# The first four heads of k through ScalarE's load queue as fp32, cast on VectorE

## The chip, the cores and the metric

The kernel runs on one core of a Trainium2 chip. The metric is the device time of one execution in microseconds (us). A profile of one execution gives, for every instruction, its engine, start and length; its span is some 1.8 us shorter than the time (572.4 us of span in a run of 574.16 us). Engines are named as in the profile: PE is TensorE's matmul side, PEld its weight load, DVE is VectorE, ACT is ScalarE, POOL is GpSimd, SP is SyncE. L147 is line 147 of the kernel.

## The reference, cut to what matters

Linformer attention over 8 batches of 8 heads (1024 tokens, head dimension 64, keys and values projected to 64 rows by E and F), then a SwiGLU feed-forward block over the 8192 resulting rows.

```python
k_proj = np.einsum('ks,bhsd->bhkd', E, k)
v_proj = np.einsum('ks,bhsd->bhkd', F, v)
scores = q @ k_proj.transpose(0, 1, 3, 2) / 8
attn = softmax(scores) @ v_proj
x = attn.transpose(0, 2, 1, 3).reshape(B * S, H * D)
out = (silu(x @ w_gate) * (x @ w_val)) @ w_out
```

## The kernel before

Everything arrives as fp32 and is computed in bf16. The loads on GpSimd's queue are cast in flight ("the casting queue" below); those on SyncE's and ScalarE's queues are not ("the hardware queues"). A load has landed when the last of its sixteen completions is there. After the first half batch of attention, PE runs the feed-forward part without a break and slips the other batches' attention in between. What matters here is the opening, before that stretch begins:

```python
load_k(0, 0, 4)                       # casting queue: heads 0 to 3 of k
for which, src in (("E", E), ("F", F)):
    nc.sync.dma_start(out=raw[:], in_=src)      # fp32, hardware queue of SyncE
...
load_k(0, 4, 8); load_q(0, 0, 2); load_v(0, (0, 4, 8)); load_w_gv(0, 1) ...   # casting queue
warm(8)                               # matmuls on zeros
turn(0)                               # transposes E on PE, ScalarE casts it to ET
turn(1)                               # transposes F on PE, VectorE casts it to FT
warm(7)
u_KV(0, "k", (0, 4), at="y")          # E times the first half of k
warm(2)
u_KT(0, at="v", prs=(0, 2))           # transposes the product
warm(2)
u_KV(0, "k", (4, 8), at="y")          # E times the second half of k
...                                   # transposes of q, scores, softmax on VectorE and GpSimd
u_KV(0, "v", (0, 4), at="y"); ... u_KV(0, "v", (4, 8), at="y")
...                                   # attention times v, then the first feed-forward matmuls
```

`warm(n)` issues n matmuls on zeros into a bank of PSUM (the memory that PE writes its results to) of the group "v". Its purpose is to keep TensorE's clock up while PE waits. PE executes all of this in program order.

The softmax here doesn't subtract the row's maximum and nothing guards it: scores larger than these inputs give would overflow.

Of the kernel before, what the change touches and what calls it, by code (L numbers as in the profile page):

```python
# [12 lines left out]
BF16 = mybir.dt.bfloat16  # L13
FP32 = mybir.dt.float32

B = 8
H = 8
S = 1024
D = 64
# [3 lines left out]
P = 128  # L23
NJ = S // P
# [10 lines left out]
def kernel(  # L35
# [19 lines left out]
    nc = tc.nc  # L55
# [4 lines left out]
    kv_pool = ctx.enter_context(tc.tile_pool(name="kv", bufs=2))  # L60
    q_pool = ctx.enter_context(tc.tile_pool(name="qbf", bufs=4))
    aw = ctx.enter_context(tc.tile_pool(name="aw", bufs=2))
# [20 lines left out]
    kb, vb, qb, xT, hT = {}, {}, {}, {}, {}  # L83

    def load_k(b, h0=0, h1=H):
        if h0 == 0:
            kb[b] = kv_pool.tile([P, H, NJ, D], BF16, name="kb", tag="kb")
        nc.gpsimd.dma_start(  # L88
            out=kb[b][:, h0:h1].rearrange("p h j d -> p h (j d)"),
            in_=k[b, h0:h1].rearrange("h (p j) d -> p h (j d)", j=NJ),  # L90
        )

    def load_v(b, heads=(0, H)):
        t = kv_pool.tile([P, H, NJ, D], BF16, name="vb", tag="vb")
        vb[b] = t
        for h0, h1 in zip(heads, heads[1:]):
            nc.gpsimd.dma_start(
                out=t[:, h0:h1].rearrange("p h j d -> p h (j d)"),
                in_=v[b, h0:h1].rearrange("h (p j) d -> p h (j d)", j=NJ),
            )  # L100
# [11 lines left out]
    def load_w_gv(c0, c1, which=(0, 1)):  # L112
        cs = slice(c0 * P, c1 * P)
        for wsrc, wdst in [((moe_w_gate, wg), (moe_w_val, wv))[i] for i in which]:
            nc.gpsimd.dma_start(
                out=wdst[:, :, cs],
                in_=wsrc[:, cs].rearrange("(t p) c -> p t c", p=P),
            )
# [11 lines left out]
    def bank(where, shape, dt, name):  # L130
        pool, tag = banks[where]
        return pool.tile(shape, dt, name=name, tag=tag)

    def copy(eng, out, in_):
        (nc.scalar.copy if eng is nc.scalar else eng.tensor_copy)(out=out, in_=in_)  # L135
# [51 lines left out]
    def u_T(b, u, at="a", eng=nc.scalar):  # L187
        ch, w = divmod(u, 4)
        g, i = divmod(w, 2)
        ps = bank(at, [P, 4, P], BF16, "qTp")  # L190
        src = qb[b, ch]
        for n in range(4):
            nc.tensor.transpose(  # L193
                out=ps[:, n, :],
                in_=src[:, 4 * g + n, 2 * i : 2 * i + 2, :].rearrange("p j d -> p (j d)"),
                identity=ident_bf[:],
            )
        t = aw.tile([P, 4, P], BF16, name="qT", tag="qT", bufs=4)
        copy(eng, t[:], ps[:])
        qT[b, u] = t  # L200
# [46 lines left out]
    def u_N(b, u):  # L247
        ch, w = divmod(u, 4)
        g, i = divmod(w, 2)
        if (b, ch) in BY_DMA:  # L250
            if (b, ch, "d") not in AA:
                AA[b, ch, "d"] = aw.tile([P, 4, H, KP], BF16, name="AAd", tag="AAd")
            a = AA[b, ch, "d"][:, 2 * i : 2 * i + 2, 4 * g : 4 * g + 4, :]
        else:
            a = AA[b, u] = aw.tile([P, 2, 4, KP], BF16, name="AA", tag="AA", bufs=4)
            a = a[:]
        eng = nc.vector if b == 0 and u in (2, 3) else nc.gpsimd
        eng.tensor_tensor(  # L258
            out=a.rearrange("p j h k -> p h j k"),
            in0=ee.pop((b, u))[:],  # L260
            in1=rr.pop((b, u))[:].unsqueeze(3).to_broadcast([P, 4, 2, KP]),
            op=ALU.mult,
        )
# [160 lines left out]
            fn(*a)  # L424

    with tc.manual_schedule():
        load_k(0, 0, 4)
        ef = []
        for which, src in (("E", E), ("F", F)):
            raw = const.tile([KP, S], FP32, name=f"{which}raw")  # L430
            nc.sync.dma_start(out=raw[:], in_=src)
            ef.append(raw)
        zeros = const.tile([P, CW], BF16, name="zeros")
        nc.vector.memset(zeros[:], 0.0)
        make_identity(nc, ident_fp[:])
        make_identity(nc, ident_bf[:])
        for i in range(2):
            nc.vector.memset(BD[i][:], 0.0)
            nc.vector.memset(BDV[i][:], 0.0)

        def turn(which):
            for half in range(2):
                ps = bank("v", [P, 4, KP], FP32, "efp")
                for i in range(4):
                    j = 4 * half + i
                    nc.tensor.transpose(
                        out=ps[:, i, :],
                        in_=ef[which][:, bass.ds(j, P, step=NJ)],
                        identity=ident_fp[:KP, :KP],
                    )  # L450
                js = slice(4 * half, 4 * half + 4)
                copy((nc.scalar, nc.vector)[which], (ET, FT)[which][:, js, :], ps[:])

        def warm(n):

            ps = bank("v", [P, CW], FP32, "warm")
            for _ in range(n):
                nc.tensor.matmul(
                    out=ps[:], lhsT=zeros[:, 0:P], rhs=zeros[:],
                    start=True, stop=True,  # L460
                )


        load_k(0, 4, 8)
        load_q(0, 0, 2)
        load_v(0, (0, 4, 8))
        load_w_gv(0, 1)
        load_w_gv(1, 2)
        load_w_gv(2, 4)
        warm(8)  # L470
        turn(0)
        turn(1)
        warm(7)
        u_KV(0, "k", (0, 4), at="y")
        warm(2)
        u_KT(0, at="v", prs=(0, 2))
        warm(2)
        u_KV(0, "k", (4, 8), at="y")
        warm(2)
        u_KT(0, at="v", prs=(2, 4))  # L480
        u_T(0, 0, "a", nc.scalar)
        u_T(0, 1, "a", nc.vector)
        u_T(0, 2, "a", nc.scalar)
        u_S(0, 0, "g")
        u_T(0, 3, "v", nc.vector)
        u_S(0, 2, "g")
        u_S(0, 1, "a")
        u_S(0, 3, "a")
        u_R(0, 0)
        u_N(0, 0)  # L490
        u_R(0, 2)
        u_N(0, 2)
        load_w_gv(4, 6, (0,))
        u_KV(0, "v", (0, 4), at="y")
        warm(1)
        u_A(0, 0, nc.scalar)
        u_R(0, 1)
        u_N(0, 1)
        u_R(0, 3)
        u_N(0, 3)  # L500
        u_A(0, 2, nc.scalar)
        u_KV(0, "v", (4, 8), at="y")
        load_w_gv(4, 6, (1,))
        load_q(0, 1)
        load_w_gv(6, 8)
        load_w_gv(8, 10)
        load_w_gv(10, 12)
        load_wo(0)
        load_wo(1)
        load_k(1)  # L510
        warm(1)
        u_PV2(0, 0, 0, 0, nc.scalar)
        u_PV2(0, 0, 1, 0, nc.vector)
        u_A(0, 1, nc.scalar)
        u_A(0, 3, nc.vector)
        f_mm(0, 0, 0, 0)
        f_mm(0, 0, 1, 0)
        u_PV2(0, 0, 0, 1, nc.scalar)
        u_PV2(0, 0, 1, 1, nc.vector)
        f_mm(0, 1, 0, 0)  # L520
        f_mm(0, 1, 1, 0)

        for i, u in enumerate(range(4, 8)):
            put(12 + i, u_T, 0, u)
            put(14 + i, u_S, 0, u)
            put(15 + i, u_R, 0, u)
            put(15 + i, u_N, 0, u)
            put(19 + i, u_A, 0, u, nc.scalar)
        put(21, u_PV, 0, 1, 0)
        put(22, u_PV, 0, 1, 1)  # L530
        put(23, u_PV, 0, 1, 2)
        put(23, u_PV, 0, 1, 3)
        put(20, load_q, 1, 0)
        put(20, load_v, 1)
        put(20, load_q, 1, 1)
        for b in range(1, B):
            place(b)
        for b in range(2, B):
            s0 = 48 * (b - 1) - (12 if b == 2 else 24)
            put(s0, load_k, b)  # L540
            put(s0 + 2, load_v, b)
            put(s0 + 4, load_q, b, 0)
            put(s0 + 6, load_q, b, 1)

        for s in slots:
            slots[s].sort(key=lambda x: x[0] not in (load_k, load_v, load_q))


        ypart = defaultdict(list)
        for c in range(B * CH - 1):  # L550
            for n in range(NFT):
                f = n if c else 4 + (2 * n + 1) // 3
                ypart[(c + 1) * NFT + f].append((c, n))

        for t in range(NIT):
            c, f = divmod(t, NFT)
            i = 1 if t < 2 else None
            f_g(c, f, i)
            run_slot(2 * t)
            f_v(c, f, i)  # L560
            for a in ypart.pop(t, ()):
                f_y(*a)
            run_slot(2 * t + 1)
        for n in range(9):
            f_y(B * CH - 1, n)
        f_y_last(B * CH - 1, 3)
        assert not slots and not ypart
# [29 lines left out]
```

## Time and profile before

| | before |
|---|---|
| time, median of the first 3 runs | 573.41 us |
| span of the profiled run | 572.4 us |
| PE busy | 98% |
| first k matmuls / second k matmuls start | 9.74 / 12.29 us |
| second half of v lands, its matmuls start | 20.01, 20.05 us |
| first feed-forward matmuls start | 22.57 us |

The lines behind these rows are in the prediction below. The first feed-forward matmuls (`gps<-xT,wg`) start at 22.57 us, and from there to the end of the span it is 572.4 - 22.57 = 549.8 us.

### The profile page before, as it was taken

What the parts mean: (1) busy time and instruction counts of PE and PEld (TensorE: products, weight loads), DVE (VectorE), ACT (ScalarE), POOL (GpSimd) and SP (SyncE); (2) the same over time, 40 slices, a digit from 0 to 9 for tenths busy, and PEclk for the clock granted to TensorE, in tenths of its full rate; (3) what the DMA queues carried; (4) which work ended last, traced back from release to release, by engine and by line L of the source; (5) the groups of instructions that cost most, each with busy time, mean ns of one, the idle gap of its engine ahead of it and who ended that gap; (6) DMA issues with size and microseconds to landing.
All of it is one profiled execution on the core that took longest, in us unless ns stands there. A gap on an engine that the chain in (4) does not pass through costs nothing.

```text
span 572.4 us, 7867 instructions
## 1 busy us (share of the span) xinstructions
PE 561.2 (98%) x2910; PEld 268.6 (47%) x2967; DVE 336.8 (59%) x580; ACT 237.0 (41%) x416; POOL 107.9 (19%) x121
## 2 busy tenths in 40 slices
PE   8899999999999999999999999999999999999997
PEld 4654544444444444444444444444444444444444
DVE  2787566666466744766556665567546674554550
ACT  1655444353425434444335434354342543443232
POOL 6734131234002400124001330023200220000000
PEclk9999999999999999999999999999999999999999
DMA  9999993539901698037951399204990124100012
GB/s 160 196 200 206 201 161 74 93 64 196 201 37 41 110 190 157 18 75 129 187 108 38 59 179 195 63 22 88 197 176 37 42 52 74 38 37 25 31 39 92
DMA packets 105927, 61.34 MB, mean 107 GB/s; under 512 B 58016, under 2 KB 97696, under 8 KB 105888
## 3 DMA queue, kind: packets, MB, share of 16 engines
q0 software_dynamic: 42288, 29.89, 36.1%
q1 hardware_dynamic: 63312, 30.68, 25.1%
q8 instruction: 23, 0.38, 0.3%
q10 hardware_dynamic: 288, 0.26, 0.1%
q14 instruction: 16, 0.13, 0.1%
HBM read 60.29 MB, written 16.78 MB: 135 GB/s over the span
## 4 chain that ended last, share of the span: by engine, by line
PE 94%; DMA 2%; POOL 1%; ACT 1%; issue 1%; DVE 0%; POOLq 0%
PE yps L360 29%; PE vps L322 29%; PE gps L322 29%; PE kvp L147 3%; PE sc L227 2%; DMA vb<-in_v_dram 2%; PE pv L285 2%; PE aTp L274 0%; ACT xT L135 0%; PE qTp L193 0%; POOL kb L88 0%; PE kTp L172 0%; POOL qb L107 0%; ACT th L334 0%; PE pv L300 0%
## 5 line engine op out<-in xcount | busy, mean ns | idle before, releaser
L341 DVE SCALAR_TENSOR_TENSOR s<-th,gps 128x512 f32<-128x512 f32 x192 | 130.5, 680 | 138.0 <-ACT th L334 137.8
L322 PE MATMUL gps<-xT,wg 128*128 128x512 bf16 (+1 forms) x755 | 195.7, 377 | 1.2
L322 PE MATMUL vps<-xT,wv 128*128 128x512 bf16 (+1 forms) x761 | 195.9, 377 | 0.8
L360 PE MATMUL yps<-wo,hT 128*128 128x512 bf16 (+2 forms) x761 | 191.5, 376 | 0.8
L334 ACT ACTIVATE th<-gps 128x512 f32<-128x512 f32 x192 | 114.6, 597 | 162.6 <-PE gps L322 155.1
L346 DVE TENSOR_TENSOR hT<-s,vps 128x512 bf16<-128x512 f32 x192 | 132.0, 688 | 22.1 <-PE vps L322 1.5
L360 PEld LDWEIGHTS <-hT 128*128 128x128 bf16 x780 | 76.2, 98 | 89.9
L258 POOL TENSOR_TENSOR AAd<-ee,rr 128x512 bf16<-128x512 f32 x52 | 54.1, 1040 | 319.5 <-issue 168.4
L322 PEld LDWEIGHTS <-wv 128*128 128x128 bf16 x776 | 73.9, 98 | 82.9 <-issue 3.3
L322 PEld LDWEIGHTS <-wg 128*128 128x128 bf16 x776 | 74.0, 98 | 81.3 <-issue 0.6
L370 ACT ACTIVATE ysb<-yps 128x512 f32<-128x512 f32 (+1 forms) x65 | 38.4, 590 | 78.1 <-PE yps L360 74.4
L135 ACT CAST xT<-pv 128x512 bf16<-128x512 f32 x62 | 36.1, 585 | 51.3 <-PE pv L285 50.3
L242 DVE TENSOR_REDUCE zz<-ee 128x8 f32<-128x512 f32 x64 | 43.5, 679 | 17.9 <-ACT ee L231 17.9
L231 ACT ACTIVATE ee<-sc 128x512 f32<-128x512 f32 x64 | 37.9, 595 | 17.4 <-PE sc L227 17.4
L285 PE MATMUL pv<-AT,BDV 128*128 128x512 bf16 x60 | 22.6, 379 | 0.1
L227 PEld LDWEIGHTS <-qTd 128*128 128x128 bf16 x208 | 16.0, 98 | 12.3
L227 PE MATMUL sc<-BD,qTd 128*128 128x128 bf16 x208 | 20.1, 219 | 0.1
L135 DVE CAST BDV<-kvp 64x256 bf16<-64x256 f32 x14 | 6.0, 426 | 22.1 <-ACT ks L157 19.1
L258 POOL TENSOR_TENSOR AA<-ee,rr 128x512 bf16<-128x512 f32 x10 | 10.3, 1038 | 35.2 <-DVE rr L244 33.6
L147 PE MATMUL kvp<-kb,ET 128*64 128x512 bf16 (+1 forms) x72 | 15.5, 357 | 1.3 <-DMA kb<-in_k_dram 1.3
L244 DVE RECIPROCAL rr<-zz 128x8 f32<-128x8 f32 x64 | 13.0, 203 | 6.2
L147 PE MATMUL kvp<-vb,FT 128*64 128x512 bf16 (+1 forms) x72 | 15.5, 358 | 1.0 <-DMA vb<-in_v_dram 1.0
(49 smaller groups left out, 144.8 us busy)
## 6 DMA issues: line engine op xcount, KB each, us to landing
out_dram<-ysb SPq DMA_DIRECT2D x63, 256.0 KB, 2.3
qb<-in_q_dram POOLq DMA_DIRECT2D x15, 512.0 KB, 16.6
kb<-in_k_dram POOLq DMA_DIRECT2D x7, 1024.0 KB, 11.6
vb<-in_v_dram POOLq DMA_DIRECT2D x7, 1024.0 KB, 14.2
wo<-in_moe_w_out_dram POOLq DMA_DIRECT2D x2, 768.0 KB, 14.8
wg<-in_moe_w_gate_dram POOLq DMA_DIRECT2D x5, 256.0 KB, 10.4
wv<-in_moe_w_val_dram POOLq DMA_DIRECT2D x5, 256.0 KB, 10.4
kb<-in_k_dram POOLq DMA_DIRECT2D x2, 512.0 KB, 8.7
```

What stands on the lines that cost most here:

```text
L135: (nc.scalar.copy if eng is nc.scalar else eng.tensor_copy)(out=out, in_=in_)
L147: nc.tensor.matmul(out=t[lo : lo + 64, h0:h1].rearrange("p h d -> p (h d)"), lhsT=w[:, j, :], rhs=src[b][:, h0:h1, j, :], start=(j == 0), ...
L227: nc.tensor.matmul(out=ps[:, n, :], lhsT=t[:, n, :], rhs=BD[b % 2][:, 4 * g + n, :], start=True, stop=True)
L231: nc.scalar.activation(out=e[:].rearrange("p h j k -> p (h j k)"), in_=ps[:].rearrange("p a k -> p (a k)"), func=AF.Exp, scale=scale,)
L242: nc.vector.reduce_sum(out=z[:], in_=e[:], axis=AX.X)
L258: eng.tensor_tensor(out=a.rearrange("p j h k -> p h j k"), in0=ee.pop((b, u))[:], in1=rr.pop((b, u))[:].unsqueeze(3).to_broadcast([P, 4, 2 ...
L322: nc.tensor.matmul(out=ps[:, ts], lhsT=(wg, wv)[w][:, kt, f * P : (f + 1) * P], rhs=x[:, kt, ts], start=(kt == 0), stop=(kt == NKT - 1),)
L334: nc.scalar.activation(out=th[:], in_=ps[:], func=AF.Tanh, scale=0.5)
L341: nc.vector.scalar_tensor_tensor(out=s1[:], in0=th[:], scalar=1.0, in1=g[:], op0=ALU.add, op1=ALU.mult)
L346: nc.vector.tensor_tensor(out=hT[c][:, f, :], in0=s1[:], in1=ps[:], op=ALU.mult)
L360: nc.tensor.matmul(out=yy[c][:, cs], lhsT=hT[c][:, f, i * P : (i + 1) * P], rhs=wo[:, f, cs], start=(f == 0), stop=(f == NFT - 1),)
L370: nc.scalar.activation(out=ysb[:, cs], in_=yy[c][:, cs], func=AF.Copy, scale=0.5)
```

## The change

The intent is to take one of the casting queue's chunks off that queue. Heads 0 to 3 of k are read raw, as two fp32 loads on ScalarE's queue, at the same moment as E and F on SyncE's. VectorE casts them. The casting queue starts with heads 4 to 7, so everything in it should come one chunk earlier. The waits of PE should shrink with that, so seven warming matmuls are taken out of them; three are put in further on.

```diff
-        load_k(0, 0, 4)
         ... (the tile kb[0] is now made here and not in load_k)
+        kraw = [aw.tile([P, 2, NJ * D], FP32, name="kraw", tag=tag) for tag in ("qTd", "AAd")]
+        for i in range(2):
+            nc.scalar.dma_start(
+                out=kraw[i][:],
+                in_=k[0, 2 * i : 2 * i + 2].rearrange("h (p j) d -> p h (j d)", j=NJ),
+            )
         ... (E and F on SyncE's queue, as before)
+        load_k(0, 4, 8)
         ...
-        load_k(0, 4, 8)
+        for h in range(4):
+            copy(nc.vector, kb[0][:, h].rearrange("p j d -> p (j d)"), kraw[h // 2][:, h % 2])
         ...
         turn(1)
-        warm(7)
+        warm(1)
         u_KV(0, "k", (0, 4), at="y")
         warm(2)
         u_KT(0, at="v", prs=(0, 2))
-        warm(2)
+        warm(1)
         u_KV(0, "k", (4, 8), at="y")
         ... (one and two warming matmuls added further on)
```

More of the change, by code (lines that the diff above doesn't have):

```diff
@@ L85, in load_k @@
     def load_k(b, h0=0, h1=H):
-        if h0 == 0:
+        if b:
             kb[b] = kv_pool.tile([P, H, NJ, D], BF16, name="kb", tag="kb")
@@ L426 @@
     with tc.manual_schedule():
-        load_k(0, 0, 4)
+        kb[0] = kv_pool.tile([P, H, NJ, D], BF16, name="kb", tag="kb")
+        kraw = [aw.tile([P, 2, NJ * D], FP32, name="kraw", tag=tag) for tag in ("qTd", "AAd")]
[4 more added lines that the diff above has]
+            )
         ef = []
@@ L482 @@
         u_T(0, 1, "a", nc.vector)
+        warm(1)
         u_T(0, 2, "a", nc.scalar)
@@ L492 @@
         u_N(0, 2)
+        warm(2)
         load_w_gv(4, 6, (0,))
```

## The prediction

> **What bounds the kernel now.** I read the page first. The tensor engine (PE) is busy for 98% of the span, and the chain that ended last is 94% PE. So the span is a long full stretch of PE plus whatever stands in front of it. The change touches only the opening, so the question is how far into the span the full stretch begins, and what sets that moment.
>
> The table of windows, cut where PE's inputs land, shows where PE is not full:
>
> ```profile
> core 0: us, PE busy (x) PEld busy (x) DVE busy (x) ACT busy (x) POOL busy (x), PEclk, DMA share, GB/s
> 0.00:9.74 9.74, 7.38 (x31) 3.73 (x32) 2.63 (x7) 2.03 (x3) 7.25 (x16) 1.00 0.82 141
> 9.74:12.29 2.55, 2.27 (x15) 1.20 (x15) 0.74 (x4) 0.37 (x1) 0.74 (x1) 1.00 1.35 196
> 12.29:14.97 2.68, 2.13 (x19) 1.44 (x20) 1.00 (x5) 0.95 (x2) 1.48 (x2) 1.00 1.34 203
> 14.97:20.05 5.08, 3.68 (x41) 2.75 (x41) 4.27 (x11) 4.09 (x10) 2.54 (x3) 1.00 1.41 197
> 20.05:26.88 6.83, 6.49 (x56) 5.21 (x58) 4.05 (x7) 3.60 (x8) 6.41 (x8) 1.00 1.53 193
> 26.88:50.00 23.12, 22.82 (x138) 11.77 (x141) 18.43 (x32) 14.98 (x28) 11.73 (x13) 1.00 1.34 202
> ```
>
> From 26.88 us on PE is 99% full (22.82 of 23.12); before that it is not, and part of what it does is warming matmuls on zeros. The same rows show transfers of 193 to 203 GB/s from 9.74 us on, but only 141 before: the DMA runs at a steady limit, except at the start.
>
> The chain of waits of the first 30 us names the limit:
>
> ```profile
> 1.28 0.90 POOL kb L88
> 3.28 0.71 POOL kb L88
> 3.99 1.49 POOL qb L107 x2
> 6.18 13.83 DMA vb<-in_v_dram
> 20.05 1.07 PE kvp L147 x8
> ```
>
> The end goes back to the second half of v, which lands at 20.05 us. It waits 13.83 us in the casting queue behind k, q and the first half of v. The PE timeline shows the whole row of landings:
>
> ```profile
> 9.74 1.03 PE L147 MATMUL kvp<-kb,ET 128*64 128x256 bf16 x8 [1.04 <-DMA kb<-in_k_dram]
> ...
> 12.29 1.03 PE L147 MATMUL kvp<-kb,ET 128*64 128x256 bf16 x8 [0.27 <-DMA kb<-in_k_dram]
> ...
> 14.97 0.40 PE L193 MATMUL qTp<-ident_bf,qb 128*128 128x128 bf16 x4 [0.40 <-DMA qb<-in_q_dram]
> ...
> 17.50 1.03 PE L147 MATMUL kvp<-vb,FT 128*64 128x256 bf16 x8 [0.61 <-DMA vb<-in_v_dram]
> ...
> 20.05 1.06 PE L147 MATMUL kvp<-vb,FT 128*64 128x256 bf16 x8 [0.41 <-DMA vb<-in_v_dram]
> ```
>
> Each half of k or v (1 MB of fp32 read, 0.5 MB of bf16 written) takes the queue 2.55 us: 12.29 less 9.74, and 20.05 less 17.50. At every landing PE stood waiting, so the opening is a conveyor belt paced by DMA. All PE's waits for DMA from the second landing on are 0.3 to 0.6 us: compute is only just behind the belt, with little slack if it alone becomes late.
>
> **What the skill says.** "DMA: Bandwidth & Descriptors", section "Issuing engines are not separate DMA queues": transfers from ScalarE, SyncE and GpSimd run on the same 16 DMA engines and interleave, so a second queue adds no bandwidth. The trace agrees: in the stretch from 4 to 6 us both the hardware queue (36 packets) and the casting queue (249) are served. A second queue can thus gain only what the engines leave unused. The same page, "SWDGE vs HWDGE vs iDMA", says a cast in flight is possible only from GpSimd; hence the raw fp32 and the VectorE casts. It gives a first byte of about 0.6 us (hardware) and 1 us (GpSimd). In the trace the first E packet starts at 2.22 us, 1.5 us after its issue at 0.74, and the first k packet about 3.6 us, 2.4 us after its issue at 1.25: longer than stated, but in the same order. "VectorE: DVE Perf Modes", errata section: a copy inside SBUF takes 58 + FD/Accel cycles at 0.96 GHz, with fp32 copies doubled. For 512 columns that is an estimate of (58+256)/0.96 = 0.33 us. No instruction of this shape is in the trace; the nearest, a bf16 copy of 128x512 from PSUM, took 0.42 us.
>
> **The change part by part.**
>
> *Removed from the casting queue:* one of its chunks, 2.55 us of the belt. If nothing else slowed, k's second half, q, v and the weights would all land 2.55 us earlier. That is the ceiling of the gain.
>
> *Added to the hardware queues:* two loads of 0.5 MB fp32, beside E and F (0.5 MB together). The cost is contention. Before, E and F packets run from 2.2 to about 4.6 us, at some 200 GB/s, half of the 410 GB/s of fp32 read that one belt chunk (1 MB in 2.55 us) shows possible. The casting queue's first packets come at 3.6. So from 2.2 to 3.6 the engines can carry perhaps 350 GB/s (a choice, between 200 and 410), 0.5 MB in all. The other 1.0 MB of the hardware loads shares the engines with k's second half, 1 MB read: 2.0 MB at 410 GB/s is 4.9 us, so both are through about 8.5 us.
>
> Landings lag the last packet. Before, the first chunk has its 512 packets started by 7.6 us but its last completion is at 9.7, because one of the sixteen completions comes over a microsecond after most others. The same 2.1 us puts k's second half at 10.6 instead of 12.29. This is a gain on the belt of about 1.65 us: 2.55 less 0.9 of contention. From there the belt's steps are as before (12.29 to 20.05 is 7.76 us), so v's second half is expected about 18.4.
>
> *Added on VectorE:* four casts, 4 x 0.33 = 1.3 us. Two can run while the second raw load is on its way, so 0.7 us lies after its landing. Then VectorE does the two FT casts (0.86 us for both). The first must free a bank before the one remaining warming matmul can run, so the first k matmuls start about 0.7 + 0.43 + 0.25 = 1.4 us after the second raw landing. The hardware loads' lag is shorter (F: last packet ends near 5.1 us, landing at 5.66). With fair sharing the second raw half lands between 7.2 and 8.2; middle 7.7. So first k matmuls start at 9.1 instead of 9.74. Behind them are 2.0 us until PE can take the second half: before it is 9.74 to about 11.94, less one warming matmul of 0.22. That makes 11.1, against 10.6 for the data. So the second half's matmuls begin at about 11.1, **1.2 us earlier** than 12.29.
>
> *Moved:* GpSimd's later issues come one issue (0.76 us) earlier; they were not the limit, as they run far ahead of the belt. *Warming matmuls:* six fewer, one fewer, then one and two more, each 0.22 us warm: all stand in PE waits. "TensorE: Matmul & The Clock Gate", Part 1, says the clock halves when idle for a window of about 3.4 us. In the trace the first eight matmuls are spaced 0.43 us and the last seven about 0.24; the idle gaps left by the change should be nearer 1 us, so I expect no slow stretch.
>
> Behind the opening, PE has no DMA wait in any view after 22 us. So what is gained in the opening comes off the end one for one: 573.4 less 1.2 to 1.3 is **572.1 us**.
>
> **The rivals.** *1. The engines are already full.* If the raw loads merely displace k's second half, it lands near 12 us and the gain is zero to 0.5 us: 573.2. Against it: 141 GB/s in the first 9.74 us against about 200 later. *2. The cast path becomes the wait.* If ScalarE's loads are issued after its table load (0.74 to 2.02 us) or lose the sharing, the second raw half lands at 9 us or later and the k matmuls start at or after the old 9.74; the time is 573.4 to 574. For it: little slack in the row of landings. Against: the loads stand first in ScalarE's program and need nothing. *3. The full chunk is gained.* If the slow first stretch comes from something the added traffic fills, the shift is 2.3 to 2.5 us: 571.0. For it: the GB/s digits dip near 7 to 8 us (107 GB/s), unused capacity. *4. VectorE's softmax row is the next limit.* Its reduces, reciprocals and multiplies stand almost without a break from 16.52 to 21.77 us. It starts from q and k, which move too, so I expect a slide, not a bound.
>
> **Range and chances.** From rival 3 to a mild case of rival 2, with 0.3 us of scatter (before: 573.11 to 574.0): 570.9 to 573.3 should hold it 8 times in 10. The 2% limits are 11.5 us away, more than four times the ceiling of 2.55 us; no step reaches them.
>
> **What will show it.** Right: the second v matmuls start near 18.4 to 18.9 us instead of 20.05, PE full from about 25.6 instead of 26.88, and the first 9 us above 141 GB/s. The casts near 0.33 us each, done by about 8.5. Wrong: k's first matmuls later than 9.74 (rival 2), k's second half landing above 11.5 (rival 1), cold matmuls of 0.43 us spacing after 8 us, or a new PE wait after 27 us that returns the gain.

## The result, and the profile after

The changed kernel is correct and took 574.63 us (median of 4 runs, 574.34 to 574.81), against 573.26 us (4 runs) for the kernel before: the ratio is 1.0022, 95% interval 1.0005 to 1.0039. Ratios here are of the fast runs' mean times, so they are not quite the ratio of the medians quoted. It became slower by about 1.3 us where 1.2 to 1.3 us of gain were forecast. In a later job it took 575.15 us against 572.95 us, ratio 1.0037 (1.0023 to 1.0052).

The PE timeline of the changed kernel, opening only. Columns: start, time taken, engine and line, operation, output and inputs, shapes, count, and the wait ahead of it with what ended it.

```profile
1.19 3.60 PE L466 MATMUL warm<-zeros 128*128 128x512 bf16 x8 [1.19 <-DVE zeros L442]
5.66 1.11 PE L454 MATMUL efp<-ident_fp,Eraw 64*128 64x64 f32 x8 [0.87 <-DMA Eraw<-in_E_dram]
8.60 1.12 PE L454 MATMUL efp<-ident_fp,Fraw 64*128 64x64 f32 x8 [1.83 <-DMA Fraw<-in_F_dram]
9.79 0.58 PE L466 MATMUL warm<-zeros 128*128 128x512 bf16 x1
10.31 1.92 PE L147 MATMUL kvp<-kb,ET 128*64 128x256 bf16 x8
12.15 1.03 PE L466 MATMUL warm<-zeros 128*128 128x512 bf16 x2
...
13.61 1.06 PE L147 MATMUL kvp<-kb,ET 128*64 128x256 bf16 x8
...
20.24 0.40 PE L274 MATMUL aTp<-ident_bf,AA 128*128 128x128 bf16 x4 [0.15 <-DVE AA L258]
20.57 1.06 PE L147 MATMUL kvp<-vb,FT 128*64 128x256 bf16 x8
...
23.08 0.73 PE L322 MATMUL gps<-xT,wg 128*128 128x256 bf16 x4
```

Three things are to be seen. The wait that was on k and v is gone, and in its place PE waits for E (0.87 us) and above all for F (1.83 us); before, it waited for neither. The eight k matmuls take 1.92 us where they took 1.03, and two warming matmuls 1.03 where they took 0.61: TensorE works at half speed. And v's second matmuls no longer stand behind a DMA wait, but start later (20.57 against 20.05).

The chain of waits of the changed kernel says the same of the path that set the end:

```profile
1.38 7.09 DMA Fraw<-in_F_dram
8.60 0.69 PE efp L454 x4
9.31 0.44 DVE FT L135
9.79 0.58 PE warm L466
10.38 1.85 PE kvp L147 x8
```

It goes back to F, issued at 1.38 and landed at 8.47 us, a matrix that is not needed before v. PE transposes it ahead of the k matmuls because the program says so. One warming matmul stands in between because it needs a PSUM bank that VectorE's FT cast must first empty.

But F came last by little. VectorE's timeline has the casts of the second raw half right ahead of the FT cast:

```profile
8.24 0.91 DVE L135 CAST kb<-kraw 128x512 bf16<-128x512 f32 x2 [2.93 <-DMA kraw<-in_k_dram]
9.31 0.86 DVE L135 CAST FT<-efp 128x256 bf16<-128x256 f32 x2 [0.15 <-PE efp L454]
```

The casts ended at 9.15 us. So with an early F the FT cast, and with it the first k matmuls, would have come only 0.15 us sooner. In the repeat of this kernel that wait is 0.60 us.

From 13.61 on, the loss shrinks. VectorE's softmax row (reduces, reciprocals, multiplies) begins at 17.51 instead of 16.52 us, 1.0 us later, and it, no longer v's landing, sets the pace, so that the feed-forward part starts 0.5 us later than in the first profile of before (23.08 against 22.57). That first profile is of a slow run of before, 574.16 us; against its two others, in the table below, the part starts 1.2 and 0.8 us later. The table of windows shows the opening as a whole; the columns are the window, its length, the busy time of each engine with its instructions, PE's granted clock, DMA share and GB/s:

```profile
0.00:10.31 10.31, 6.34 (x26) 3.06 (x26) 4.51 (x11) 2.03 (x3) 7.39 (x16) 1.00 0.90 217
10.31:13.61 3.30, 3.30 (x15) 1.58 (x14) 0.22 (x1) 0.36 (x1) 1.94 (x3) 1.00 1.36 200
13.61:20.57 6.96, 6.66 (x65) 4.36 (x65) 5.36 (x15) 4.57 (x10) 2.08 (x3) 1.00 1.49 194
20.57:27.40 6.83, 6.65 (x60) 5.21 (x58) 4.41 (x9) 4.06 (x9) 6.22 (x8) 1.00 1.37 183
27.40:50.00 22.60, 22.30 (x135) 11.39 (x138) 18.21 (x31) 14.54 (x28) 11.33 (x14) 1.00 1.33 201
```

The DMA did what was hoped, in part: 217 GB/s in the first ten microseconds instead of 141, at a busy share of 0.90 instead of 0.82. The GB/s flatter the change, because the trace counts a casting load by the bf16 bytes that it writes (512 packets of 1024 bytes for 1 MB read) and a raw load by its fp32 bytes. PE is busy for only 6.34 us of 10.31, and busy for all of 10.31 to 13.61, where it works slowly. The clock column gives 1.00 for both rows. It shows no value below 1 until the first record of a change, and in this trace the first record, of full clock, comes at 13.16 us; what was before it has to be read from the length of the matmuls.

How the loads were served, by queue, from the DMA view of the window from 2 to 6 us (q0 is the casting queue, q1 SyncE's, q10 ScalarE's; packets, MB, share of the engines' time). The kernel before:

```profile
q1 hardware_dynamic: 160, 0.52, 51.0%
q0 software_dynamic: 261, 0.27, 46.5%
```

The changed kernel:

```profile
q10 hardware_dynamic: 499, 0.99, 75.3%
q1 hardware_dynamic: 91, 0.31, 22.4%
```

There is no line of q0 at all. The casting queue's load of k was issued at 1.25 us in both kernels; before, 261 of its packets had been served by 6 us, now none. Packet by packet the trace shows the order, by the starts of each load's first and last packet: the first raw load 1.81 to 3.69 us, E 3.51 to 4.38, the second raw load 4.21 to 6.80, F 5.76 to 7.22, and the casting queue's first load 6.40 to 9.57. The loads did not share the engines evenly; they were served nearly one after another.

The Trainium skill has this in "DMA: Bandwidth & Descriptors", "Queues, rings and completion order": an engine takes turns between its queues by packets of some 9 to 17 descriptors. A raw load of 256 packets has 16 for each of the 16 engines. If the trace's packets are the page's descriptors, its whole share is about one such turn: an estimate that fits the order above, not a proof. I had cited this page for the sharing and assumed the fair division of single packets. Why the casting queue gets nothing before 6.40 us is not explained by the page or by any run here.

### The profile page after: what moved, and what is told of

Same layout as the page of the kernel before. It is cut to its first block, busy times and chain, and to the rows that moved or that the text cites. A ratio compares the mean times of both kernels' runs of the same rounds, so it can differ in the third digit from the quotient of the medians.

```text
span 572.9 us, 7867 instructions
## 1 busy us (share of the span) xinstructions
PE 562.2 (98%) x2907; PEld 268.3 (47%) x2963; DVE 338.6 (59%) x584; ACT 236.9 (41%) x416; POOL 107.3 (19%) x120
## 4 chain that ended last, share of the span: by engine, by line
PE 94%; DVE 2%; DMA 1%; ACT 1%; issue 1%; SPq 0%; DVEq 0%
PE yps L360 29%; PE vps L322 28%; PE gps L322 28%; PE kvp L147 3%; PE sc L227 2%; PE pv L285 2%; DMA Fraw<-in_F_dram 1%; DVE zz L242 1%; PE qTp L193 1%; PE warm L466 0%; DVE s L341 0%; DVE hT L346 0%; PE kTp L172 0%; ACT xT L135 0%; PE aTp L274 0%
## 5 line engine op out<-in xcount | busy, mean ns | idle before, releaser
L227 PEld LDWEIGHTS <-qTd 128*128 128x128 bf16 x208 | 16.0, 98 | 12.3
## 6 DMA issues: line engine op xcount, KB each, us to landing
kb<-in_k_dram POOLq DMA_DIRECT2D x7, 1024.0 KB, 11.3
```

What stands on the lines that cost most here:

```text
L227: nc.tensor.matmul(out=ps[:, n, :], lhsT=t[:, n, :], rhs=BD[b % 2][:, 4 * g + n, :], start=True, stop=True)
```

## The experiments

Two theories and a rival. **A:** F, served last, stands ahead of k in PE's program. **B:** TensorE's clock stays at half speed, because PE idles and the warming matmuls were removed. **C (rival):** the casting queue itself was held up by contention, so nothing could be gained. All kernels give the reference's result. "FF start" is the first feed-forward matmul in the profile; the time of each kernel is to be compared with the kernel before on the same chip. The jobs of e1 to e4 ran on one chip, those of e5 to e9 and the repeats on another; there the 12 runs of before for the last job (572.95) are the 11 of the job ahead of it (573.08) and one more.

| run | 2nd k matmuls | 2nd half of v lands | FF start | time | before, same chip | ratio (95%) |
|---|---|---|---|---|---|---|
| before, 1st profile | 12.29 | 20.01 | 22.57 | | 573.26 | |
| before, 2nd profile | 12.51 | 18.52 | 21.91 | | 573.08 | |
| before, 3rd profile | 12.02 | 19.74 | 22.29 | | 572.95 | |
| changed | 13.61 | 17.99 | 23.08 | 574.63 | 573.26 | 1.0022 (1.0005 to 1.0039) |
| changed, again | 13.58 | 17.87 | 23.60 | 575.15 | 572.95 | 1.0037 (1.0023 to 1.0052) |
| e1 turn of F late | 13.41 | 17.94 | 24.35 | 575.29 | 573.51 | 1.0033 (1.0020 to 1.0047) |
| e2 warm | 12.38 | 18.37 | 21.85 | 573.59 | 573.51 | 1.0011 (0.9996 to 1.0026) |
| e3 both | 12.14 | 18.29 | 21.61 | 573.34 | 573.51 | 1.0005 (0.9991 to 1.0018) |
| e4 loads only | 16.50 | 21.03 | 25.89 | 577.34 | 573.51 | 1.0067 (1.0055 to 1.0079) |
| e5 both, turn of F between | 11.81 | 18.12 | 21.29 | 572.69 | 573.08 | 0.9994 (0.9982 to 1.0006) |
| e6 and F issued last | 11.51 | 18.18 | 20.98 | 572.63 | 573.08 | 1.0000 (0.9987 to 1.0013) |
| e7 before, 1 for 7 warm | 12.48 | 19.01 | 21.88 | 572.44 | 573.08 | 0.9989 (0.9976 to 1.0002) |
| e8 and 4 for 9 warm | 10.61 | 18.11 | 20.67 | 572.59 | 572.95 | 0.9991 (0.9978 to 1.0004) |
| e9 before, warm 10 and 4 | 11.04 | 18.55 | 21.10 | 573.21 | 572.95 | 1.0003 (0.9990 to 1.0016) |

The landings of v are the last of the load's sixteen completions in the trace.

**e1: the turn of F moved back, nothing else.**

```diff
         turn(0)
-        turn(1)
         warm(1)
         u_KV(0, "k", (0, 4), at="y")
         warm(2)
         u_KT(0, at="v", prs=(0, 2))
+        turn(1, "g")                     # another PSUM group
```

> The changed kernel, with the transposes of F moved from before the first k matmuls to behind the first k transposes, in another PSUM bank; nothing else. Theory A (F, which now lands at 8.5 us instead of 5.7 us, holds up PE in program order): the first k matmuls start about 9.3 us instead of 10.3 us, the opening gets about 1 us shorter than in the changed kernel, time about 573.6 us. Theory B (the cold TensorE clock is what costs): the k matmuls still take 1.9 us for 8, and less than half of the loss comes back. Theory C (the casting queue itself was slowed by contention): no change.

The first k matmuls did start earlier, at 8.97 us, but it did not help: 575.29 us. The PE timeline of this run:

```profile
8.97 1.86 PE L147 MATMUL kvp<-kb,ET 128*64 128x256 bf16 x8 [1.46 <-DVE kb L135]
...
13.41 1.92 PE L147 MATMUL kvp<-kb,ET 128*64 128x256 bf16 x8
```

Both k groups are slow now (1.86 and 1.92 us), the clock's record of full speed comes only at 16.76 us, and the turn of F now delays the second group. So the expectation of 573.6 us was wrong: F's place alone is not the cause, and with a cold clock removing that wait gains nothing.

**e2: warming matmuls put back into the two waits.**

```diff
-        warm(8)
+        warm(10)
         turn(0)
+        warm(4)
         turn(1)
         warm(1)
```

> The changed kernel with warming matmuls put back into PE's two waits: ten instead of eight ahead of the turn of E, and four between the turns of E and F. Theory B (cold clock): the first 8 k matmuls take 1.03 us instead of 1.92 and the two warming matmuls behind them 0.6 instead of 1.03, so the second k matmuls start near 12.3 us instead of 13.6 although F lands as late as before; time about 573.4 us. Theory A alone: the k matmuls still start at 10.3 us and the time stays within 0.3 us of the changed kernel.

Theory B's numbers came nearly to the digit. The PE timeline of this run:

```profile
8.92 1.07 PE L454 MATMUL efp<-ident_fp,Fraw 64*128 64x64 f32 x8 [0.83 <-DMA Fraw<-in_F_dram]
...
10.37 1.06 PE L147 MATMUL kvp<-kb,ET 128*64 128x256 bf16 x8
...
12.38 1.06 PE L147 MATMUL kvp<-kb,ET 128*64 128x256 bf16 x8
```

F's transposes start no earlier than before the edit (8.92 against 8.60 us), the first k matmuls start at the same time (10.37 against 10.31), and yet the second start at 12.38 instead of 13.61 and the feed-forward part at 21.85 instead of 23.08: 1.23 us, at full clock. The time, 573.59 us, is the same as that of the kernel before. So in the profile keeping the clock up is enough to take the loss away, with F as late as it was. The times alone do not separate e2 from the changed kernel: their intervals overlap (0.9996 to 1.0026, and 1.0005 to 1.0039 or 1.0023 to 1.0052).

**e3: both edits** (ten warming matmuls, nine behind the turn of E, turn of F as in e1).

> Both edits together (turn of F late; PE kept warm until the raw k is cast). If A and B are the two causes and the belt of the casting queue did gain its 2 us: first k matmuls near 9.3 us at full clock, second k matmuls near 11.3 us against 12.3 in the kernel before, time about 572.3 us, 1 us below the kernel before. If VectorE's softmax row has become the limit for another reason, it stays above 573 us.

573.34 us, not 572.3: with the clock held, F's place is worth a further 0.24 us in the profile (21.85 to 21.61). The first k matmuls started at 9.24 as expected, the second at 12.14 and not 11.3, since the turn of F was now in front of those. This was a flaw of the edit, mended in e5.

**e4: contention alone.** The kernel before, with the two raw loads added on ScalarE's queue and never used.

```diff
         load_k(0, 0, 4)
+        kraw = [aw.tile([P, 2, NJ * D], FP32, name="kraw", tag=tag) for tag in ("qTd", "AAd")]
+        for i in range(2):
+            nc.scalar.dma_start(out=kraw[i][:], in_=k[0, 2 * i : 2 * i + 2]...)
```

> The kernel before with the two raw fp32 loads of k added on ScalarE's queue and not used: contention alone. If the raw loads are served ahead of the rest, E and F land about 1 and 2.8 us later and the casting queue's first chunk lands at about 12.3 instead of 9.7 us, with every later landing 2 to 2.5 us later: time about 575.5 us. If the engines had the room, landings move by under 0.5 us and the time stays at 573.3.

577.34 us, more than either figure. E landed at 5.98 and F at 9.02 us, 1.5 and 3.4 us later than in the first profile of before (1 and 2.8 expected in the first case); the casting queue's first chunk landed at 10.76 us, not 12.3, where five profiles without raw loads have 7.90 to 9.70, mean 8.80. The second half of v came at 21.03 against a mean of 19.17. So the raw loads cost the casting queue about 1.9 us of the 2.55 us that taking a chunk away gives. The rest of the rise is on PE's side: F and the seven warming matmuls behind it stand ahead of the k matmuls, F's transposes start at 9.15 us instead of 5.86, and the warming matmuls are cold (3.15 us from 10.34 on, against 1.67). How much of it is F and how much the clock was not separated. Rival C is thus partly right: the engines have only a little room. It is not the reason for the loss, as v still lands earlier in the changed kernel.

**The kernel before, profiled again, twice.**

> The kernel before once more, for a second profile. Its times scatter over 1.7 us in the first study (572.59 to 574.27) while its profile is of a run of 574.2. If the scatter comes from the opening, the first matmuls of the feed-forward part start at another time than 22.57 us, by as much as the time differs; if from elsewhere, they start at 22.57 us.

> The kernel before, a third profile. In the first, the first k half landed at 9.7 us and the second v half at 20.0; in the second, 7.9 and 18.5. If the first profile was the unusual one, this run is near the second (first k half before 9 us, second v half before 19.2); if the spread is even, anything between.

The first expectation holds: the feed-forward part starts 0.66 and 0.28 us earlier than in the first profile, and the two runs took 0.65 and 0.27 us less. In these three runs the opening makes the scatter. For the landings, the third profile came near the first and not the second, so the first was not an oddity. The five profiles with the casting queue as before (three of before, e7 and e9) have the first k half at 9.70, 7.90, 9.43, 8.71 and 8.24 us, and the second half of v between 18.52 and 20.01. The profile that the prediction was made from is the latest of the five. In it one of the sixteen completions of that first load comes 1.2 us after all others, in the third three come a microsecond after the rest; in the second all sixteen lie within 0.6 us. The eight profiles of the change and its variants (e4 apart) have v between 17.87 and 18.37. The second profile shows a second cause of scatter. Its table of windows, same columns as above:

```profile
4.00:7.39 3.39, 2.92 (x20) 2.20 (x19) 0.80 (x2) 0.74 (x2) 3.39 (x5) 1.00 1.17 188
7.39:10.80 3.41, 3.41 (x12) 1.44 (x10) 0.05 (x1) 0.00 (x0) 1.79 (x3) 0.50 1.25 192
10.80:14.00 3.20, 3.20 (x21) 1.52 (x19) 0.89 (x4) 0.73 (x2) 1.78 (x3) 1.00 1.37 201
```

The clock is at half for 3.41 us although PE is never idle in that window; in the one ahead of it PE was busy for 2.92 of 3.39 us. The kernel before, too, is sometimes cold in its opening, and whether it is differs between executions of the same program.

**e5: turn of F between the first k matmuls and their transposes,** in place of two warming matmuls, with e3's warming.

> As the run with both edits, but with the turn of F put between the first k matmuls and their transposes, in place of two warming matmuls, so that PE does it while ScalarE copies. Theory (F in program order and the cold clock are all that keeps the casting queue's 2 us from the end): second k matmuls near 11.4 us instead of 12.14, first feed-forward matmuls near 20.9 instead of 21.6 us, time near 572.7 us. Rival (VectorE's softmax row or the weights' landing is already the limit): first feed-forward matmuls stay near 21.6 us.

Second k matmuls at 11.81 (11.4 expected), feed-forward at 21.29 (20.9 expected), 572.69 us (572.7 expected). The rival, a fixed limit near 21.6, is out: the profile is below it.

**e6: as e5, and F issued last,** third on ScalarE's queue instead of second on SyncE's.

> As the run before it, with F issued third on ScalarE's queue, behind both raw loads of k, instead of second on SyncE's. Theory (the engines serve whole loads nearly one after the other, in turn between the queues): the second raw half of k lands near 7 us instead of 8.4, F near 8.5 as before; k matmuls start near 8 us, second half of k (10.3 to 10.6) is then the limit, first feed-forward matmuls near 20.3 us, time near 572.1 us. Rival (loads share the engines packet by packet): the landing of the raw half hardly moves, and neither does the time.

The second raw half landed at 7.09 us instead of 8.61, with F at 9.35: which load is served when depends on the order of issue, as this run's theory says. The rival, an even sharing, is out. The k matmuls did not start at 8 us, though, but at 9.11: nine warming matmuls, put there to fill the wait, ran until then. The time, 572.63 us, missed the 572.1 expected; two of its six runs were at 574.1 and 574.3, at a granted clock of 1.0, and I did not find out why.

**e7: the kernel before, with the change's one warming matmul for seven.**

> The kernel before with one part of the change alone: one warming matmul instead of seven between the turn of F and the first k matmuls. If the missing warming matmuls alone make the clock cold: the first k matmuls take 1.9 us for 8 instead of 1.03, the second k matmuls start near 13.1 instead of 12.29 us, and the time rises by 0.5 to 1 us. If PE's wait here (2.8 us) is too short to cool it: no change; then it takes the added waits of the changed kernel too.

A miss in part. The first k matmuls were cold (1.75 us for 8), but the second started at 12.48 and the median did not rise: 572.44 us. The profile is of the slowest of the five runs (573.52 us). In it PE took k's second half 1.2 us after its landing at 11.25, and the feed-forward part starts 2.87 us after v's landing (21.88 - 19.01), where it is 2.56 us when PE waits for v (22.57 - 20.01). So the cold stretch of one window cost at most some 0.3 us there; the rest of it was hidden. Of the other four runs, three have the same mean clock of 0.997 and took 572.3 to 573.0 us. So it takes the change's added waits for E and F, together with fewer warming matmuls, to make the clock cold for so long that it is on the path.

**a2: the changed kernel again.**

> The changed kernel again, beside the others of this job. If its loss is the cold clock and F's place, it is so in every run: k matmuls of 0.24 us each near 10.3 us, first feed-forward matmuls near 23.1 us, time 574.3 to 574.8 us, while the kernel before stays at 572.6 to 574.

575.15 us, and the feed-forward part at 23.60: both a little later than expected, and again slower than the kernel before. Here the trace has the clock's records, so that the table of windows shows what the first profile could not:

```profile
4.49:7.90 3.41, 1.28 (x9) 0.96 (x8) 1.22 (x3) 0.74 (x2) 3.41 (x6) 1.00 1.10 275
7.90:14.73 6.83, 6.35 (x28) 3.64 (x29) 2.26 (x8) 0.37 (x1) 3.05 (x4) 0.50 1.32 202
14.73:18.00 3.27, 3.21 (x37) 2.07 (x35) 1.74 (x6) 2.04 (x5) 0.00 (x0) 1.00 1.36 199
```

In the first window PE is busy for 1.28 us of 3.41: it waits for E and then F. Then the clock is at half for 6.83 us, two windows of 3.41, through both groups of k matmuls. The Trainium skill, "TensorE: Matmul & The Clock Gate", Part 1, says that the clock is judged in free-running windows of 3.41 us. The trace agrees: the cold stretches in these records last 3.41 and 6.83 us. It also means that a wait shorter than a window can cost a window, which is what I had not reckoned with. In all four runs of this job the changed kernel had a mean granted clock of 0.994. In the first profile of it no full clock is recorded before 13.16 us, and it may never have had it before: E's transposes took 1.11 us there, as F's did at half clock in the repeat, and 1.06 us at full clock.

Cut into windows of 3.41 us at the clock's records, the first 22 us of the fourteen profiles show more. Four windows at full clock were followed by half clock; PE was busy in them for 1.28 us (this run), 1.06 (e4), 1.94 (e7) and 2.94 (the second profile of before). Others kept full clock with less, down to 2.23 us (the third profile of before). So busy time alone does not decide. Without the fp32 transposes of E and F the four have 0.22, 0.00, 0.53 and 0.81 us, and every window that kept full clock has about 1.2 us or more. That those transposes do not keep the clock up is inferred from these figures; no run was made to test it.

**e8: as e6, with four warming matmuls instead of nine** behind the turn of E.

> As the run with F issued last, but with four instead of nine warming matmuls behind the turn of E, since the raw half of k now lands at 7.1 us and PE was still warming until 9.1. Theory (PE's own program is the limit there): k matmuls near 8.0 us, second k matmuls near 10.5 us, when that half lands; first feed-forward matmuls near 20.2 to 20.9 us instead of 20.98; time 572.0 to 572.6 us. Rival: the clock goes cold again, matmuls of 0.24 us, and the time rises above 573 us.

The PE timeline of this run:

```profile
8.15 1.03 PE L147 MATMUL kvp<-kb,ET 128*64 128x256 bf16 x8
...
10.61 1.06 PE L147 MATMUL kvp<-kb,ET 128*64 128x256 bf16 x8
...
18.16 1.06 PE L147 MATMUL kvp<-vb,FT 128*64 128x256 bf16 x8 [0.43 <-DMA vb<-in_v_dram]
...
20.67 0.72 PE L322 MATMUL gps<-xT,wg 128*128 128x256 bf16 x4
```

Now v's landing sets the pace again, at 18.16, and the step from there to the feed-forward part is 20.67 - 18.16 = 2.51 us, as it was before (22.57 - 20.05 = 2.52). In this profile, of the fastest of its four runs (572.24 us), the casting queue's gain has reached the end: 2.4 us less opening than the changed kernel, 1.2 to 1.9 us less than the three profiles of before. The median is 572.59 us against 572.95. The interval of the ratio, 0.9978 to 1.0004, still contains 1, so this form is the best of the variants of the change, but I cannot call it faster than the kernel before.

**e9: the kernel before, with ten and four warming matmuls.**

> The kernel before with ten and four warming matmuls instead of eight and seven, and no other edit. If the kernel before too loses time to a clock that goes cold in its opening (as in its second profile, between 7.4 and 10.8 us), it keeps full clock here, the first feed-forward matmuls start at 21 to 22 us, and the time is 572.3 to 572.9 us: then the best form of the change gains next to nothing over the kernel before. If not, it stays at 573.1 to 573.5 us.

In the profile it works: full clock, feed-forward at 21.10 us. In the times it does not show: 573.21 us, with two runs at 572.7 and two at 573.7 and 574.0. The scatter that comes from the first landing remains. e9 is also the fair comparison for e8, as both keep full clock and wait for v: e8's opening is 0.43 us shorter in the profiles (20.67 against 21.10), as much as v landed earlier (18.11 against 18.55). The times of the two, four runs each, overlap (572.2 to 573.0, and 572.7 to 574.0).

## Why the prediction was wrong

**Right.** The opening is all that moves, and it moves the end one for one: the remainder was 549.8 us in each profile. The casting queue did move up: k's second half landed at 10.24 us (10.6 predicted), v's second half at 17.99 (18.4 predicted). That these came so close is partly luck, because two errors cancelled: the last packet of k's second half started at 9.57 us, where all was to be through by 8.5, and it landed 0.7 us later, where 2.1 us of lag were taken over from one late completion. The added traffic filled part of the slow start (a DMA share of 0.90 against 0.82). "Same" within 2% was right. The warning that compute was "only just behind the belt, with little slack if it alone becomes late" is what came true. Of the signs of being wrong that were named beforehand, two were seen: k's first matmuls later than 9.74 us, and cold matmuls after 8 us.

**Wrong, the step that failed.** The failed step reads: "the idle gaps left by the change should be nearer 1 us, so I expect no slow stretch". The gaps were 0.87 us for E and 1.83 us for F, and TensorE ran at half clock until 13.16 us (in the repeat from 7.90 to 14.73). By e2, which restores only the clock, this is worth 1.23 us at the second k matmuls and at the feed-forward part. It is enough to turn the result around.

**The start of the k matmuls.** I followed the raw halves of k through the contention and never F, which was taken as landed at 5.66 us. It landed at 8.47, and the chain of waits goes back to it. But little of the late start is F's: the first k matmuls started at 10.31 and not 9.1, and of these 1.2 us some 0.5 are the second raw half (8.22 instead of 7.7), 0.2 its casts (0.91 instead of 0.7), 0.15 the wait for F, and 0.3 the FT cast and the warming matmul behind it, which took 1.0 us (9.31 to 10.31) instead of 0.68; the warming matmul was cold (0.58 us, against 0.38 in e2). From the first k matmuls to the second it took 3.30 us instead of 2.0, and 2.01 in e2, so these 1.3 us are the clock's. Together they are the 2.5 us between the second k matmuls as predicted (11.1) and as measured (13.61). e1 takes F's turn and the FT cast out of the way (k matmuls at 8.97) and gains nothing, because the clock is then cold for longer and the turn delays the second group.

**Mis-sized terms.** "With fair sharing" was not what happened: the loads were served one after another. The second raw half came at the late end of the range all the same (8.22, and 7.49 in the repeat, for 7.2 to 8.2). The casts took 0.50 us each at the median (0.41 to 0.64; their records overlap, and a pair took 0.91 to 0.96) instead of 0.33; the working had left out that the cited section itself calls its fixed term of 58 cycles too low (see the end). The contention was put at 0.9 us of the 2.55; the unused loads of e4 cost about 1.9 us. The low figure came from comparing with a profile in which the first chunk landed at 9.70 us, the latest of five: the gain in v's landing was 2.0 us against that profile, but about 1.1 us against the mean of five (19.17 to a mean of 18.09 in the changed kernel, its repeat, e1, e2 and e3).

**The rivals.** The nearest is rival 2, the cast path as the new wait, but by another mechanism: ScalarE's loads were issued at 0.74 us, ahead of its table load, and the raw half was cast 0.15 us before the chain through F was ready for VectorE. By that little it was not what PE waited for. Rival 4 was dismissed too early: once the k matmuls were late, VectorE's softmax row took over from v's landing as the limit.

**Open.** Why the casting queue is not served before about 6 us when both hardware queues are used. What TensorE's clock counts as activity. Why the casting queue's first load sometimes has one or a few completions that come a microsecond late. Why single runs of e2, e3, e6 and e9 are some 1 to 3 us slower than their fellows; in one such run of e2 the mean granted clock was 0.994, in the others mostly 1.0.

## What to carry to other kernels

When loads are moved from one queue to another, follow every load that shares the engines, not only the moved ones, and look at where each consumer stands in an in-order engine's program: the least urgent load may hold up the most urgent work. Count the waits of TensorE that a change creates at the place where it takes warming matmuls away; here waits of 0.94 and 1.60 us were followed by two windows at half clock. And profile a kernel more than once before sizing a gain of a microsecond: here the first landing alone differed by 1.8 us between profiles of the same loads.

## What the Trainium skill lacked or had wrong

- "DMA: Bandwidth & Descriptors": it says that the engines take turns between queues, not that a casting load can be left unserved: with both hardware queues used, the first packet of the one issued at 1.25 us started at 6.40 us, against 3.56 us, and 261 packets by 6 us, with one hardware queue used.
- The same page gives first-byte latencies of about 0.6 us (hardware) and 1 us (GpSimd): counted from the start of the issuing instruction, E's first packet started 1.5 us after it in the kernel before, the first raw load's 1.1 us after it in the changed kernel, and k's in the casting queue 2.3 us after it in the kernel before.
- "VectorE: DVE Perf Modes", errata section: its formula gives an estimate of 0.33 us for a copy of 512 fp32 columns inside SBUF, at the doubled rate that the page's tier table has for fp32; pairs of such casts to bf16 took 0.76 to 1.06 us in these runs, so 0.38 to 0.53 each. The section is not wrong in this: it says itself that the formula is too low for VectorE and that about 150 cycles were measured in place of the 58, which gives an estimate of (150 + 256)/0.96 = 0.42 us.
- "TensorE: Matmul & The Clock Gate": the window of 3.41 us agrees with the records. The rule of its section on HAM oscillation, to avoid idle gaps of over 3.4 us, is too weak here: in the repeat of the changed kernel, with waits of 0.94 and 1.60 us and transposes in between, PE was busy for 1.28 us of a 3.41 us window, and two windows at half clock followed. The page does say that many short idles can have this effect, but not how much activity a window needs, nor whether fp32 transposes count: here windows with at most 0.81 us of other matmuls lost full clock, and those with about 1.2 us or more kept it.
